# Weight conversions begun behind the 40th exponential instead of the 19th, and the MLP's work beside the attention eleven units later

## The chip, the cores and the metric

The kernel runs on one core of a Trainium2 chip. A core has TensorE (PE) for matrix products, VectorE (DVE), ScalarE (ACT), GpSimd (POOL) and SyncE (SP), whose queue issues the transfers. What is measured is the device time of one execution in microseconds, median of the runs.

## The reference, cut to what matters

Rotary attention, then two MLPs, each over the output of the one before:

```python
q_rot, k_rot = rotate(q), rotate(k)                # 4 batches, 8 heads, 576 tokens, 64 wide
attn = softmax(q_rot @ k_rot.T / sqrt(64))
x = (attn @ v)  ->  2304 tokens x 512
h = x @ w_in                                       # 512 x 2048
g = where(h >= 1, h, where(h <= -1, 0, (h + 1)**2 / 4))
x = g @ w_out                                      # 2048 x 512
h = x @ w_in2
out = (s * max(h, 0)**2 + b) @ w_out2
```

The MLP weights come as 64-bit floats.

## The kernel before, in words

Every matrix product of the MLPs is made of three: each operand is split into a high part (the operand cast to the fp32r type) and a low part, the rest, and high by high, high by low and low by high are summed. Turning one half (512 columns) of a weight slice from 64-bit floats into these two parts is a **conversion** (`Slice.convert`, called by `half`). It loads 512 KB (`load`, line 145), and then takes two ACT steps (line 134 at its start, line 139 for the high part), four DVE steps (lines 135 to 138, of 128 x 512) and two differences or sums on POOL, which the helper `pool_tt` (line 96) cuts in two pieces each (tiles `wm` and `w`). The raw data has two buffers, the scratch tiles `wa` and `wm` one.

The attention goes through 16 pairs of heads (`NPAIR`), four pairs for each batch, and each pair has nine **units** (`UNITS`), 144 in all. A unit takes its scores on TensorE (line 357), their maximum on DVE (`nm`, line 359), the exponential on ACT (`p`, line 364, kept in `exps`), transposes of the result (line 379) with copies by ACT or DVE, and, twice in a pair, the product with the values (`av`, lines 405 to 412). The scores have two buffers, and one comes free when its exponential is done. The rotation of the next pair's queries and keys (`rope_pair`, `lay_q`, `lay_k`) runs on POOL, DVE and ACT beside it (tiles `qin`, `kin`), and the laid keys go by transfers to `kh` and `kz`.

The unit loop traces, for each n, the five steps of `ORDER`: scores of unit n, loads and conversions (`do_load`), transposes, value products, and fill (`do_fill`). `issue_after(ins)` puts the instructions traced in its block behind `ins`, but only those on that instruction's own engine; for an exponential that is ACT. A planner then orders every engine's instructions ahead of time, by the order in which they were traced and by when it expects them to be ready, so an instruction may be issued before or behind others of its engine where no such bound stands. After that each engine takes its queue in order.

The **fill** is work of the first MLP that needs only tokens whose batch is finished. `beside(work)` is a generator for each batch but the last, and three shares come out of `ORDERS`: 2, 6 and 2 items. It issues the load and split of its first block of 288 tokens (`split_x`: tiles `xs`, `xh`, `xl`), then yields `LEAD` times with no work, and then one yield for each MLP unit: four first-layer units (`h`, 12 matmuls of line 181, and the activation) and four second-layer units (`y`, again 12 matmuls, line 181) for each item, 80 units in all. The first-layer units need the first half of four slices converted, the second-layer units the second half. `run_fill(budget)` takes steps from the generators:

```python
    def do_fill(n):
        if n < 48:
            return
        with tc.issue_after(exps[min(n, len(units)) - 4]):
            run_fill(0.62 if n < 76 else 0.92)
```

The loop runs n to 147, and `while fill: run_fill(1.0)` behind it traces what is left. A share is appended when the value product of its batch's last pair is traced, at n = 41, 75 and 111, and shares are taken one after the other.

Sixteen conversions prepare the eight slices of `set_a`, first halves and second halves of four slices and then of the other four. `convert()` takes the next. Nine of its calls stand at n = 33, 35, ... 49, the others at n = 70, 74, ... Eight more halves of later slices are converted and parked in memory from n = 96 on (`PARK_AT`). Behind the attention, `stage` goes on with the first MLP over the rest of the tokens (`hps`, `yps`), and the second MLP follows.

Of the kernel before, what the change touches and what calls it, by code (L numbers as in the profile page):

```python
# [36 lines left out]
RB = 2  # L37
XB = 3
N2 = 464
LEAD = 4  # L40
LT = 2
LA = 4
PB = 3
# [23 lines left out]
def kernel(ctx, tc, qq, kk, vv, tab, ww1, ww2, s, b, out):  # L67
# [45 lines left out]
    exps, tps, maxs = {}, {}, {}  # L113

    class Slice:
# [6 lines left out]
        def convert(self, raw, pools, hi, lo):  # L122
            if not wide:
                split(hi, lo, raw, nc.scalar, nc.gpsimd)
                return


            top = raw.bitcast(F32).rearrange("p (n t) -> p n t", t=2)[:, :, 1]
            low = raw.bitcast(U16).rearrange("p (n t) -> p n t", t=4)[:, :, 1]
            pool = pools[self.f * 2 + self.made & 1 if len(pools) > 1 else 0]  # L130
            a = pool.tile([P, HW], F32, tag="wa", name="wa", bufs=WB)
            m = pool.tile([P, HW], F32, tag="wm", name="wm", bufs=WB)
            au, mu = a.bitcast(U32), m.bitcast(U32)
            nc.scalar.activation(a, top, AF.Copy, scale=2.0 ** -112)
            nc.vector.tensor_scalar(out=mu, in0=au, scalar1=3, scalar2=None, op0=ALU.logical_shift_left)
            nc.vector.scalar_tensor_tensor(out=mu, in0=au, scalar=0x80000000, in1=mu, op0=ALU.bitwise_and, op1=ALU.bitwise_or)
            nc.vector.tensor_scalar(out=au, in0=mu, scalar1=0xFF800000, scalar2=None, op0=ALU.bitwise_and)
            nc.vector.scalar_tensor_tensor(out=a, in0=low, scalar=2.0 ** -36, in1=a, op0=ALU.mult, op1=ALU.mult)
            nc.scalar.copy(hi, m)  # L139
            pool_tt(out=m, in0=m, in1=hi, op=ALU.subtract)  # L140
            pool_tt(out=lo, in0=m, in1=a, op=ALU.add)
# [116 lines left out]
    def load_qk(i, nm, pieces=WHOLE):  # L258
        bb, hp = divmod(i, NP)
        t = att2.tile([P, 2, S], F32, tag="qkin", name=f"{nm}in", bufs=QB)  # L260
        for c in pieces:
            nc.sync.dma_start(out=t[:, :, c], in_=(qq if nm == "q" else kk)[bb, hp, :, :, c])
        qk_in[nm, i] = t

    def load_v(i):
        bb, hp = divmod(i, NP)
        t = att2.tile([P, 5, 2, D], F32, tag="vin", name="vin", bufs=VB)
        for out, src in ((t[:, :, 1], vv[bb, hp, :, :, 1]), (t[:D, :4, 0], vv[bb, hp, D:, :4, 0]), (t[D:, :4, 0], vv[bb, hp, :D, 1:, 0]), (t[D:, 4, 0], vv[bb, hp, :D, 0, 0])):
            nc.sync.dma_start(out=out, in_=src)
        v_in[i] = t  # L270
# [15 lines left out]
    def rope_pair(i, nm, mul, add, lo_eng, pieces=WHOLE):  # L286

        t = qk_in[nm, i]
        tt = {nc.gpsimd: pool_tt, nc.vector: nc.vector.tensor_tensor}
        last = None  # L290
        for c in pieces:
            tt[mul](out=t[:, :, c], in0=t[:, :, c], in1=tab_sb[:, :, c], op=ALU.mult)
            r = t[:, 1, c]
            tt[add](out=r, in0=t[:, 0, c], in1=r, op=ALU.add)
            last = (lay_q if nm == "q" else lay_k)(i, t, c, lo_eng)
        return last
# [4 lines left out]
    def lay_q(i, t, c, lo_eng, heads=range(2)):  # L301

        st = stacks["q", i] = qs_t[i % 2]
        r = t[:, 1, c]
        for j in heads:
            own, other = SELF[j], SELF[1 - j]
            at = slice(j * QW + c.start, j * QW + c.stop)
            h = nc.scalar.activation(st[own, at], r[own], AF.Copy, scale=0.125)
            m = nc.vector.scalar_tensor_tensor(out=st[other, at], in0=r[own], scalar=0.125, in1=st[own, at], op0=ALU.mult, op1=ALU.subtract)
        return h.ins, m.ins  # L310
# [153 lines left out]
    def split_x(c, again):  # L464
        xh = m1.tile([P, KD, N1], F32R, tag="xh", name="xh")
        xl = m1.tile([P, KD, N1], F32R, tag="xl", name="xl")
        if again:
            return load_parts((xh, xl), c * N1, N1)
        for k in range(KD):
            xs = m2.tile([P, N1], F32, tag="xs", name="xs", bufs=3)  # L470
            nc.sync.dma_start(out=xs, in_=xd[k, :, c * N1:(c + 1) * N1])
            split(xh[:, k, :], xl[:, k, :], xs, nc.scalar, nc.gpsimd)
        return xh, xl
# [3 lines left out]
    def beside(work):  # L477
        x = split_x(work[0][0], work[0][0] in kept)
        for _ in range(LEAD):
            yield 1.0  # L480
# [48 lines left out]
    def turned_by(t, c):  # L529
        nc.vector.tensor_tensor(out=t[:, :, c], in0=t[:, :, c], in1=tab_sb[:, :, c], op=ALU.mult)  # L530
        return nc.vector.tensor_tensor(out=t[:, 1, c], in0=t[:, 0, c], in1=t[:, 1, c], op=ALU.add).ins
# [53 lines left out]
    def do_load(n):  # L585
        if n == 0:
            with tc.issue_after(turned):
                turned_by(tq, QP[1])
                lay_q(0, tq, QP[1], None)
        elif n in (1, 2):  # L590
            with tc.issue_after(maxs[n]):
                if n == 1:
                    turned_by(tq, QP[2])
                else:
                    lay_q(0, tq, QP[2], None)
        if n < len(units):
            i, k = units[n]
            if i + 1 < NPAIR:
                if i == 0 and k in (2, 6):
                    with tc.issue_after(maxs[k]):  # L600
                        turned_by(qk_in["q", 1], HALVES[k // 6])
                if i == 0 and k in (4, 5, 7, 8):
                    with tc.issue_after(maxs[k]), tc.issue_after(exps[k - 1]):
                        lay_q(1, qk_in["q", 1], HALVES[k // 6], None, [int(k in (5, 8))])
                if i and k == 0:
                    with ExitStack() if i > 1 else tc.issue_after(parts[1][1]), ExitStack() if i > 1 else tc.issue_after(maxs[9]):
                        rope_pair(i + 1, "q", nc.gpsimd, nc.vector, None)
                elif k == 2:
                    with ExitStack() if i else tc.issue_after(exps[2]), ExitStack() if i else tc.issue_after(lowest):
                        rope_pair(i + 1, "k", nc.gpsimd, nc.gpsimd, [nc.gpsimd, nc.vector])  # L610
                elif k == 7:
                    load_v(i + 1)
                elif k in (4, 6) and i + 2 < NPAIR:
                    load_qk(i + 2, "q" if k == 4 else "k")

        if n in range(33, 51, 2) or n in range(70, 110, 4):
            with tc.issue_after(exps[n - 14]):
                convert()

        if n in PARK_AT and parking:  # L620
            with tc.issue_after(exps[n - 4]):
                parking.pop(0).park(wst, scratch)()
# [31 lines left out]
# [6 lines that stand above are left out]
    acts = {"q": do_qk, "l": do_load, "t": do_t, "a": do_av, "f": do_fill}  # L660
    for n in range(len(units) + LA):
        with ExitStack() as st:
# [541 lines left out]
```

## Time and profile before

| | us |
|---|---|
| median of 3 runs | 1116.79 |
| lowest and highest | 1115.44, 1121.0 |
| the profiled execution, its time | 1116.36 |
| its span, first to last instruction | 1114.6 |
| PE, DVE, ACT, POOL busy | 1071.6, 783.8, 626.7, 428.6 |
| first and last exponential begin | 15.2, 417.5 |
| first matmul of the fill begins | 132.9 |

The span is the time between the program's first and last instruction on the chip; the execution's own time is a little longer. Busy time of PE includes matmuls that overlap, so a PE that is always busy may still not be at its densest.

### The profile page before, as it was taken

The page shows a single profiled execution, that of the slowest core. Times are in us where ns is not written, and L with a number is a line of the kernel's source. Part 1 is how long each engine was busy: PE and PEld are TensorE (multiplying, and loading weights), DVE is VectorE, ACT ScalarE, POOL GpSimd, SP SyncE. Part 2 cuts the span into 40 slices and gives each one's busy share as a digit, 9 for nine tenths or more (in the row PEclk, how much of TensorE's full clock was granted, in tenths as well). Part 3 has the DMA queues.
Part 4 walks back from the last instruction along what each step waited for, and adds up shares of the span by engine and source line. Part 5 has one row for each costly group of instructions (what it writes and reads, how often), then busy time and mean ns, then how long its engine had stood idle before and what let it go on. Part 6 is the DMA issues. An engine that isn't in the chain of part 4 may idle for free.

```text
span 1114.6 us, 20055 instructions
## 1 busy us (share of the span) xinstructions
PE 1071.6 (96%) x7296; PEld 979.2 (88%) x7296; DVE 783.8 (70%) x1453; ACT 626.7 (56%) x1432; POOL 428.6 (38%) x564
## 2 busy tenths in 40 slices
PE   5898999999999999999999999999999999999998
PEld 4666787778888889999999999999999999999997
DVE  7989998887666663454657666867777778677754
ACT  5777877767656665454545445474555448334431
POOL 6988978785553332332544445110212110000000
PEclk9999999999999999999999999999999999999999
DMA  8665956665656544656465663231322843221220
GB/s 240 170 190 163 270 162 212 216 191 152 213 179 189 173 151 140 223 167 194 146 187 204 211 228 113 94 113 59 116 87 90 303 169 117 83 82 44 81 63 36
DMA packets 109762, 173.24 MB, mean 155 GB/s; under 512 B 29408, under 2 KB 80608, under 8 KB 109664
## 3 DMA queue, kind: packets, MB, share of 16 engines
q1 hardware_dynamic: 109664, 171.97, 49.0%
q8 instruction: 57, 0.93, 0.4%
q14 instruction: 41, 0.34, 0.1%
HBM read 110.10 MB, written 48.56 MB: 142 GB/s over the span
## 4 chain that ended last, share of the span: by engine, by line
PE 73%; DVE 8%; POOL 7%; DMA 6%; ACT 3%; issue 3%; SPq 0%; POOLq 0%; DVEq 0%; ACTq 0%
PE hps L181 14%; PE sum L940 14%; PE yps L856 6%; PE yps L854 6%; PE yps L855 6%; PE yps L790 4%; PE yps L791 4%; PE yps L792 4%; PE h L181 3%; PE sc L357 3%; PE y L181 3%; PE av L405 3%; POOL kin L96 3%; PE tp L379 2%; DVE nm L359 2%
## 5 line engine op out<-in xcount | busy, mean ns | idle before, releaser
L181 PE MATMUL hps<-xh,w 128*128 128x288 f32 (+4 forms) x640 | 163.4, 325 | 0.0
L364 ACT ACTIVATE p<-sc,nm 128x576 f32<-128x576 f32 x144 | 106.5, 741 | 40.6 <-DVE nm L359 35.7
L357 PE MATMUL sc<-kh,qs 128*128 128x288 f32 x336 | 102.6, 328 | 25.6 <-ACT p L364 14.8
L359 DVE TENSOR_REDUCE nm<-sc 128x1 f32<-128x576 f32 x144 | 106.8, 748 | 20.5 <-PE sc L357 19.8
L948 ACT ACTIVATE four<-four,b_sb,s_sb 128x480 f32<-128x480 f32 x64 | 47.4, 782 | 127.8 <-DVE four L947 127.8
L856 PE MATMUL yps<-gh,w 128*128 128x480 f32 (+1 forms) x320 | 118.6, 371 | 0.0
L854 PE MATMUL yps<-gh,w 128*128 128x480 f32 (+1 forms) x320 | 118.5, 370 | 0.0
L855 PE MATMUL yps<-gl,w 128*128 128x480 f32 (+1 forms) x320 | 118.5, 370 | 0.0
L181 PEld LDWEIGHTS hps<-xh,w 128*128 128x128 f32 x640 | 113.3, 188 | 1.0
L96 POOL TENSOR_TENSOR wm<-wm,w 128x256 f32<-128x256 f32 x80 | 67.8, 867 | 109.2 <-ACT w L139 62.3
L181 PE MATMUL hps<-xl,w 128*128 128x288 f32 (+4 forms) x320 | 103.7, 324 | 0.0
L357 PEld LDWEIGHTS sc<-kh,qs 128*128 128x128 f32 x336 | 63.3, 191 | 45.2 <-ACT p L364 26.3
L790 PE MATMUL yps<-gh,w 128*128 128x288 f32 (+3 forms) x288 | 93.2, 323 | 1.2 <-DVE yp L797 0.7
L357 PE MATMUL sc<-kz,qs 128*128 128x288 f32 x336 | 92.9, 299 | 0.0
L792 PE MATMUL yps<-gh,w 128*128 128x288 f32 (+3 forms) x288 | 92.9, 323 | 0.0
L791 PE MATMUL yps<-gl,w 128*128 128x288 f32 (+3 forms) x288 | 92.9, 323 | 0.0
L379 PE MATMUL tp<-ident,p 128*128 128x128 f32 x576 | 87.3, 276 | 2.6 <-DVE pt L386 1.8
L96 POOL TENSOR_TENSOR wm<-wm,raw 128x256 f32<-128x256 f32 x16 | 12.8, 820 | 175.1 <-ACT raw L139 175.1
L405 PE MATMUL av<-pt,vin 128*64 128x256 f32 (+1 forms) x512 | 75.1, 418 | 1.3 <-ACT pt L382 0.8
L181 PE MATMUL y<-gh,w 128*128 128x288 f32 x320 | 73.9, 303 | 1.4 <-ACT pt L382 0.4
L379 PEld LDWEIGHTS tp<-ident,p 128*128 128x128 f32 x576 | 70.1, 142 | 5.6 <-DVE pt L386 2.8
L181 PE MATMUL h<-xh,w 128*128 128x288 f32 x320 | 71.8, 301 | 2.9 <-DVE pt L386 2.1
(153 smaller groups left out, 2888.5 us busy)
## 6 DMA issues: line engine op xcount, KB each, us to landing
wraw<-in_ww SPq DMA_DIRECT2D x56, 512.0 KB, 4.2
w<-parkd SPq DMA_DIRECT2D x24, 512.0 KB, 6.1
kin<-in_k SPq DMA_DIRECT2D x15, 576.0 KB, 5.6
qin<-in_q SPq DMA_DIRECT2D x15, 576.0 KB, 5.1
kh<-kin SPq DMA_DIRECT2D x60, 144.0 KB, 3.1
parkd<-wraw SPq DMA_DIRECT2D x16, 512.0 KB, 3.2
xs<-y1d SPq DMA_DIRECT2D x32, 240.0 KB, 2.7
xd<-u SPq DMA_DIRECT2D x16, 288.0 KB, 2.6
```

The source lines that it names most:

```text
L96: m = nc.gpsimd.tensor_tensor(out=out[c], in0=in0[c], in1=in1[c], op=op)
L181: m = nc.tensor.matmul(out_ps, l, r, start=(i == 0), stop=(i == n - 1))
L357: nc.tensor.matmul(sc[:, half, o:o + n], l, r[:, k0:k0 + n], start=m == 0, stop=m == len(todo) - 1)
L359: maxs[i * 9 + k] = nc.vector.tensor_reduce(out=nm, in_=sc[:, :, :288], axis=AX.XY, op=ALU.max, negate=True).ins
L379: m = nc.tensor.transpose(v[:, c, :], p[:, c * P:(c + 1) * P], ident)
L790: nc.tensor.matmul(acc, wh, gh, start=f == 0, stop=False)
L791: nc.tensor.matmul(acc, wh, gl, start=False, stop=False)
L792: nc.tensor.matmul(acc, wl, gh, start=False, stop=last)
L854: nc.tensor.matmul(acc, wh, gh, start=f == 0, stop=False)
L855: nc.tensor.matmul(acc, wh, gl, start=False, stop=False)
L856: nc.tensor.matmul(acc, wl, gh, start=False, stop=last)
L940: nc.tensor.matmul(acc, l, r, start=j == 0, stop=j == len(t) - 1)
```

## The change

The generators of the fill yield eleven times with no work instead of four. The nine early calls of `convert` stand at n = 45, 47, ... 61, and the ACT steps of each are queued behind exponential n - 5 (the 40th to the 56th) instead of n - 14 (the 19th to the 35th). The later calls are as they were.

```diff
-LEAD = 4
+LEAD = 11
...
-        if n in range(33, 51, 2) or n in range(70, 110, 4):
-            with tc.issue_after(exps[n - 14]):
+        if n in range(45, 63, 2) or n in range(70, 110, 4):
+            with tc.issue_after(exps[n - 5 if n < 63 else n - 14]):
                 convert()
```

## Rows read from the trace of the kernel before

**Rows 1.** the page, span and busy time of each engine
```profile
span 1114.6 us, 20055 instructions
...
PE 1071.6 (96%) x7296; PEld 979.2 (88%) x7296; DVE 783.8 (70%) x1453; ACT 626.7 (56%) x1432; POOL 428.6 (38%) x564
```

**Rows 2.** windows: edges, length, busy us (instructions) per engine, clock, DMA
```profile
54.20:73.20 19.00, 18.03 (x133) 12.83 (x132) 17.36 (x29) 14.34 (x35) 14.61 (x19) 1.00 0.64 177
...
73.20:94.00 20.80, 18.84 (x137) 13.11 (x137) 18.88 (x32) 15.43 (x37) 17.86 (x26) 1.00 0.56 165
...
94.00:114.20 20.20, 18.00 (x131) 12.57 (x128) 18.37 (x30) 14.76 (x36) 17.79 (x24) 1.00 0.67 196
...
134.30:161.30 27.00, 24.70 (x193) 21.33 (x192) 24.60 (x42) 20.45 (x51) 25.71 (x34) 1.00 0.52 156
...
161.30:186.60 25.30, 23.16 (x176) 20.09 (x176) 20.03 (x35) 18.89 (x47) 17.84 (x24) 1.00 0.73 225
...
186.60:216.00 29.40, 28.10 (x227) 23.98 (x223) 24.35 (x44) 20.98 (x51) 22.84 (x30) 1.00 0.59 188
...
216.00:241.30 25.30, 22.23 (x163) 19.56 (x163) 20.89 (x37) 19.11 (x49) 19.11 (x27) 1.00 0.59 183
...
241.30:273.40 32.10, 29.43 (x231) 26.33 (x231) 24.85 (x45) 21.65 (x55) 21.83 (x29) 1.00 0.62 193
...
366.20:398.10 31.90, 31.68 (x250) 28.33 (x251) 19.02 (x38) 21.21 (x56) 12.23 (x18) 1.00 0.56 173
```

**Rows 3.** the same windows for line 357 alone, the score matmuls
```profile
73.20:94.00 20.80, 7.82 (x42) 5.76 (x42) 1.00 0.56 165
```

**Rows 4.** the same windows for line 181 alone, the MLP matmuls
```profile
134.30:161.30 27.00, 9.73 (x62) 8.31 (x61) 1.00 0.52 156
...
161.30:186.60 25.30, 9.46 (x62) 8.37 (x62) 1.00 0.73 225
...
186.60:216.00 29.40, 9.26 (x60) 8.30 (x60) 1.00 0.59 188
...
216.00:241.30 25.30, 10.52 (x68) 9.31 (x68) 1.00 0.59 183
...
241.30:273.40 32.10, 15.15 (x98) 13.43 (x99) 1.00 0.62 193
...
366.20:398.10 31.90, 16.38 (x108) 14.45 (x107) 1.00 0.56 173
```

**Rows 5.** chain of the whole run, one piece: start us, us, what
```profile
426.49 3.20 PE y L181 x24
```

**Rows 6.** chain of waits between 54 and 103 us, shares by line
```profile
by line: issue 16.6%; POOL kin L96 13.9%; DMA kz<-kin 10.5%; POOL qin L96 10.4%; POOL wm L96 6.7%; PE sc L357 6.1%; DVE nm L359 5.3%; POOL w L96 4.7%; PE av L405 3.6%; PE tp L379 3.0%; DMA kin<-in_k 2.9%; DVE wm L136 2.6%; DVE qs L309 2.5%;
```

**Rows 7.** instructions by line, 54 to 134 us: busy us, mean ns
```profile
L96 POOL TENSOR_TENSOR w<-wm,wa 128x256 fp32r<-128x256 f32 x10 | 7.9, 797 | 0.1
...
L96 POOL TENSOR_TENSOR wm<-wm,w 128x256 f32<-128x256 f32 x10 | 7.6, 779 | 1.9 <-DVE wa L137 1.9
...
L138 DVE SCALAR_TENSOR_TENSOR wa<-wraw,wa 128x512 f32<-128x512 uint16 x6 | 6.6, 1100 | 0.1
```

**Rows 8.** line 96 between 54 and 134 us, ns min/median/max
```profile
L96 POOL TENSOR_TENSOR kin<-kin,tab_sb x16: 783/801/1322, 66.8 to 126.8; 128x288 f32<-128x288 f32 x16
```

**Rows 9.** line 134, first ACT step of conversions, to 255 us
```profile
L134 ACT ACTIVATE wa<-wraw x16: 648/674/702, 55.8 to 246.0; 128x512 f32<-128x512 f32 x16
```

**Rows 10.** timeline of ACT, 110 to 186 us: start us, us
```profile
130.02 0.69 ACT L134 ACTIVATE wa<-wraw 128x512 f32<-128x512 f32 x1
...
185.18 0.69 ACT L134 ACTIVATE wa<-wraw 128x512 f32<-128x512 f32 x1
```

**Rows 11.** tile xh, 130 to 440 us: ns min/median/max, transfer landing
```profile
L96 POOL TENSOR_TENSOR xl<-xs,xh x21: 793/812/1247, 152.6 to 439.3; 128x288 fp32r<-128x288 f32 x21
...
DMA to landing us min/median/max: 3.4/4.5/8.1
```

**Rows 12.** waits of PE between 417 and 475 us
```profile
PE yps L790 <- ACT ys L507: 0.5, 1, 0.5
```

## The prediction

> **What bounds the kernel now.** I read the page first. TensorE is busy for 1071.6 of 1114.6 us, VectorE for 783.8, GpSimd for 428.6 [rows 1]. So nearly all of the span is matrix work that the change neither adds nor removes, and only stretches in which TensorE is not densely fed can pay or cost. To find them I cut the attention part into windows of nine attention units, one head pair each. The edges are the starts of every ninth exponential: 54.2 us is the 18th, 73.2 the 27th, then the 36th (94.0), 45th (114.2), 54th (134.3), 63rd, 72nd, 81st, 90th and 99th (273.4), and the row at 366.2 runs from the 126th to the 135th. Each such window holds 42 score matmuls, 4 for each of eight units and 10 for the unit of both heads' ends [rows 3].
>
> A window with MLP units in it must be freed of them before it can be compared. An MLP unit is 12 matmuls of line 181, and 24 of them took 3.20 us at a stretch [rows 5], so 1.6 us each unit where TensorE is dense. The window at 366.2 us is dense, busy 31.68 of 31.9 us [rows 2]. It holds 108 such matmuls [rows 4], 9 units or 14.4 us, which leaves **17.5 us for nine attention units, the floor**. The same subtraction over the other windows [rows 2, 4] gives 18.7 at 134.3, 17.0 at 161.3, 21.4 at 186.6, 16.2 at 216.0 and 19.0 at 241.3. The three windows with no MLP at all took 19.0, 20.8 and 20.2, mean 20.0 [rows 2]. So without filler nine units cost about 2.5 us over the floor. There VectorE is busy 91% of the time and GpSimd 77 to 88%, and TensorE's clock stays at 1.00, the level of 2.4 GHz [rows 2].
>
> Who holds up those windows? The chain of waits from 54 to 103 us runs through GpSimd's rotary work on `kin` and `qin` (24.3%), but also through the conversions: 6.7 and 4.7% in GpSimd's pieces for `wm` and `w`, 2.6% in VectorE's `wm` [rows 6]. That is 14.0% of 49 us, 6.9 us.
>
> **The change part by part.** No instruction is added or removed. Sixteen conversions of MLP weights start between 55.8 and 246.0 us [rows 9], 12.7 us apart in the mean. Four of them lie before the 40th exponential (which by the window edges starts near 103 us). The first nine now go behind the 40th to 56th, so these four leave the stretch. Their loads leave it too, from the third on, since the raw weights have two buffers and each further load waits for a conversion to end; on SyncE's queue they move behind the loads of the next pairs, and no exponential waits for them.
>
> The fill's budget follows from the code. Inside the unit loop it is 28 x 0.62 + 72 x 0.92 = 83.6 steps. Before, the first two shares take 4 + 16 and 4 + 48 of them, the third gets 11.6, 4 of them lead: 71.6 MLP units beside attention, 8.4 behind it. After, 11 + 16 and 11 + 48 are 86 already: 61.6 units beside attention, 18.4 behind. Ten units, 16 us of TensorE, move from attention to its tail; as dense work that is even, and only what each stretch loses or gains over the floor counts. The first MLP unit comes 7 / 0.62 = 11.3 units later, at the 66th instead of the 54th or 55th. The second share has a pause 7 / 0.92 = 7.6 units longer, about the 85th to the 97th. The third share's pause now lies behind the loop, where it takes no time.
>
> A, units 18 to 40 without conversions. At most the chain's 6.9 us come back, at least nothing, since GpSimd's rotary chain stands right behind. I take half, **-3.4 us**.
>
> B, units 54 to 66 without MLP, with conversions. Before, nine at 18.7 and three at the rate of 17.0, together 18.3 for nine. After, I take the 20.0 of the windows that also hold conversions and no MLP: 1.7 x 12 / 9 = **+2.3 us**. Ends: nothing, and 20.8 against 17.0, +5.1.
>
> C, the longer pause of the second share. The windows from 186.6 to 273.4 average 18.9 freed of MLP; 20.0 - 18.9 over 7.6 units is **+0.9 us**. Ends: nothing, and 20.8 against 16.2, +3.9.
>
> D, ten more MLP units behind attention. In the tail before, TensorE waited 0.5 us in all between 417 and 475 us [rows 12], because the third share's input had been loaded and split long before. Now its four transfers and splits are issued with no lead. A transfer of this tile takes 4.5 us to land, and four low parts on GpSimd 4 x 0.81 us [rows 11], 7.7 us together. The work that hides it is the 2.4 last units of the second share, 3.8 us, and the last units' transposes and value products. Without the latter 3.9 us stand open, with them none; I take **+2.0 us**.
>
> The parked weights, the next stage and everything behind it keep their work and order; the conversions end some 20 us later, while the first weights of the second half are due only after the fill's 27 + 11 + 16 steps, beyond the 110th unit. I cost them at nothing.
>
> Sum: -3.4 + 2.3 + 0.9 + 2.0 = +1.8 us. The profiled execution took 1116.36 us, 1.8 over its span and 0.4 under the median of 1116.79. That gives 1118.2 for it and, carried to the median, **1118.6**. Ends of all terms: -6.9 and +12.9.
>
> **The rivals.** First, GpSimd is the true limit and filler hides conversions later for nothing. A conversion holds GpSimd for 2 x (797 + 779) ns = 3.2 us [rows 7], and while it shares the stretch its neighbours stretch too: the rotary pieces of one shape took 783 to 1322 ns [rows 8]. The whole 6.9 us would come back and B to D be nothing: 1116.4 - 6.9 = **1109.5**. It decides once A, less B to D, is over 5.6 us. Against it: the floor leaves 2.5 us for nine units, 6 us for the 22 units, so A would have to reach the floor. The Trainium skill (SBUF — State Buffer, "Who interferes with whom") says that a VectorE instruction with two SBUF inputs and a reading GpSimd instruction exclude each other for the whole instruction; two of a conversion's VectorE steps are such, the one at line 138 with a mean of 1100 ns [rows 7], and the spread on GpSimd agrees with it. By that rule a conversion costs GpSimd up to 2.2 us more than its own pieces, which speaks for this rival and is why it has a chance above one in ten.
>
> Second, slower: the conversions come too late for the first second-layer units. These need eight. Where conversions followed one another without pause, six started from 130.02 to 185.18 us [rows 10], 11.0 us apart. Starting near 100 us, the eighth starts at 177 and is done some 8 us later, at 185. The first such unit is due after 26 units at 20.0 for nine (58 us), and 6.5 more with four MLP units (20.8 us): 179 us. The stall would be 6 us, and where the order on TensorE's queue is fixed nothing behind it can pass. 1118.6 + 6 = **1125**. It decides once the spacing is over 10.2 us. Against it: without MLP activations on the engines the spacing may shrink, and the order may be laid so that attention fills in.
>
> Third, the pauses are hidden and A is as small as they are: within a microsecond or two of before. That is the forecast's own neighbourhood, and I count it there.
>
> **How the numbers follow.** A measurement here can tell about 0.5%, 5.6 us, from no change: below 1111.2 is faster, above 1122.4 slower. The forecast (all small terms, nothing decides) 0.52, of which 0.04 spills over each bound; the first rival 0.20; the second 0.20; a tail or pause at its dear end (D or C, +5 to +12) 0.08, of which 0.02 stays within the bounds. So faster is 0.04 + 0.20 = 0.24, slower 0.04 + 0.20 + 0.06 = 0.30, and the same 0.44 + 0.02 = 0.46. The range from 1109.5, the first rival, to 1128, near the upper end of the terms, leaves out about 0.2.
>
> **What would show it.** A: the first conversion near 100 us instead of 55.8, and the 36th exponential 2 to 5 us before 94.0. B: no line 181 before some 155 us, and nine units at about 20 us up to there. C: a second stretch without line 181 near the 85th to 97th unit. D: some 18 to 20 MLP units behind the last exponential, with TensorE's waits for `xh` or `xl` there up to 4 us. The forecast is wrong if windows without MLP run near 17.5 us once conversions are gone (then faster), or if line 181's second-layer matmuls wait for conversions (then slower).

## The result, and the profile after

The changed kernel takes 1126.83 us (median of 6 runs, 1124.07 to 1130.43), the kernel before 1117.69 us beside it (6 runs). The ratio is 1.0087, 95% interval 1.0070 to 1.0105: **slower by about 9.7 us**. That lies inside the stated range, above the likeliest time by 8. The profiled execution took 1130.43 us, the slowest of the six, so sums over its trace come out some 3 or 4 us too large.

The page, span and busy time:

```profile
span 1128.7 us, 20086 instructions
...
PE 1077.5 (95%) x7296; PEld 984.6 (87%) x7296; DVE 783.2 (69%) x1453; ACT 628.4 (56%) x1432; POOL 428.6 (38%) x564
```

TensorE has the same work within 6 us [rows 1], spread over 14 us more. The windows below are nine attention units each, by the same exponentials as before: the edges are the starts of the 18th, 27th, 36th, 45th, 54th, 63rd and, last row, 90th. The columns are as in [rows 2].

```profile
57.10:74.70 17.60, 17.19 (x127) 12.18 (x124) 14.19 (x24) 13.41 (x33) 12.45 (x18) 1.00 0.48 134
...
74.70:93.70 19.00, 18.05 (x132) 12.55 (x130) 13.94 (x24) 12.67 (x31) 11.29 (x17) 1.00 0.50 141
...
93.70:116.80 23.10, 20.21 (x151) 14.18 (x151) 18.46 (x30) 15.60 (x40) 16.15 (x21) 1.00 0.61 167
...
116.80:137.60 20.80, 18.00 (x145) 13.95 (x141) 19.39 (x34) 15.53 (x37) 19.07 (x25) 1.00 0.84 258
...
137.60:160.80 23.20, 18.38 (x132) 14.99 (x132) 19.52 (x33) 15.38 (x36) 17.56 (x26) 0.93 0.60 174
...
160.80:187.50 26.70, 23.61 (x183) 20.14 (x182) 24.05 (x42) 20.17 (x52) 23.45 (x30) 1.00 0.47 138
...
243.80:269.20 25.40, 21.01 (x151) 17.00 (x150) 19.49 (x36) 16.23 (x40) 16.82 (x24) 0.93 0.61 171
```

Line 181 alone in two of them, as in [rows 4]:

```profile
160.80:187.50 26.70, 8.41 (x56) 7.66 (x56) 1.00 0.47 138
...
243.80:269.20 25.40, 2.01 (x14) 1.93 (x15) 0.93 0.61 171
```

First, units 18 to 36, now free of conversions, took 17.6 and 19.0 us against 19.0 and 20.8 [rows 2]: 3.2 us gained, and the first of them runs at the floor. The next nine, where the conversions now begin, lost 2.9 us again (23.1 against 20.2). Second, the three windows with conversions and no MLP took 23.1, 20.8 and 23.2, mean 22.4, where I had put 20.0 for those from the 54th unit on. Third, the second share's pause: 25.4 us less 14 matmuls of 181 (1.9 us) leaves 23.5 for nine units, against 19.0 before. Last, TensorE's clock column reads 0.93 in two of these rows, where it read 1.00 in every row of before.

The first step of the conversions, as in [rows 9]; 20 here, since the window is longer and holds parked ones too:

```profile
L134 ACT ACTIVATE wa<-wraw x20: 649/676/741, 102.9 to 328.2; 128x512 f32<-128x512 f32 x20
```

TensorE's largest wait between 15 and 500 us, in the changed kernel and then in the one before (total us, times, longest us):

```profile
PE sc L357 <- ACT p L364: 22.2, 22, 3.7
```

```profile
PE sc L357 <- ACT p L364: 14.8, 17, 1.9
```

Most of the extra waiting, 7.4 us, is in the scores, which wait for an exponential to free their buffer. No matmul of the fill waits for a converted weight: there is no such row in this list. Last, the tail, in windows from the last value product to about the end of the fill's last matmul, changed kernel and before:

```profile
428.60:467.00 38.40, 37.89 (x285) 37.65 (x284) 10.56 (x26) 20.39 (x58) 11.95 (x16) 1.00 0.63 200
```

```profile
432.00:456.00 24.00, 23.46 (x175) 23.23 (x176) 7.26 (x17) 13.57 (x38) 9.54 (x12) 1.00 0.72 222
```

Both are as good as full, 37.9 of 38.4 and 23.5 of 24.0 us.

**One stop followed back.** TensorE has two stops of 3.7 us. The first ends at 150.2 us. This is the chain of waits in front of it (start us, us, what):

```profile
140.27 2.85 issue
...
144.94 2.02 POOL qin L96 x2
...
146.98 1.33 DVE qin L294
...
149.35 0.84 ACT p L364 x2
...
150.23 0.81 PE sc L357 x4
```

The score waits for an exponential, that for a maximum, that stands on VectorE behind the addition `qin` of line 294, and the addition waits for GpSimd. This is the timeline of GpSimd there, with its idle time in brackets:

```profile
143.16 3.79 POOL L96 TENSOR_TENSOR qin<-qin,tab_sb 128x288 f32<-128x288 f32 x4 [2.89 <-DMA qin<-in_q]
```

GpSimd had nothing for 2.9 us because a query load had not landed. On SyncE's queue this load (line 262) was issued right behind a raw weight load (line 145):

```profile
133.24 1.27 SPq L329 DMA_DIRECT2D kz<-kin  x2
136.93 0.35 SPq L145 DMA_DIRECT2D wraw<-in_ww  x1
...
137.38 0.38 SPq L262 DMA_DIRECT2D qin<-in_q  x1
```

And this is why it was late, a row of SyncE's own waits between 100 and 160 us:

```profile
SPq L145 <- DVE wa L138: 5.4, 3, 2.7
```

The weight load stood at the head of the queue until a conversion's last VectorE step gave its buffer back (at line 138), 5.4 us in three times; here 2.4 us, from the end of the issue before it at 134.5. The query that came late belongs to a pair whose scores are due more than a dozen units later, but its addition had its place in VectorE's queue ahead of maxima that were due at once. Two windows of 5 us show what follows:

```profile
145.00:150.00 5.00, 1.58 (x14) 1.34 (x12) 3.55 (x6) 1.24 (x3) 5.00 (x6) 1.00 0.67 202
...
150.00:155.00 5.00, 4.77 (x26) 4.74 (x27) 3.25 (x6) 4.54 (x14) 4.86 (x9) 0.66 0.07 24
```

In the first, TensorE is busy for 1.6 of 5 us; in the second it has work again for 4.8 us, at a mean clock of 0.66, part of it at 1.2 instead of 2.4 GHz. The second stop, from 253.7 to 257.4 us, looks the same on VectorE, which waited 3.6 us for GpSimd in front of such an addition. What held up the query there was not followed:

```profile
254.13 1.33 DVE L294 TENSOR_TENSOR qin<-qin 128x576 f32<-128x576 f32 x1 [3.62 <-POOL qin L96]
```

### The profile page after: what moved, and what is told of

Read it like the earlier page. It is cut to its first block, busy times and chain, and to the rows that moved or that the text cites. A ratio compares the mean times of both kernels' runs of the same rounds, so it can differ in the third digit from the quotient of the medians.

```text
span 1128.7 us, 20086 instructions
## 1 busy us (share of the span) xinstructions
PE 1077.5 (95%) x7296; PEld 984.6 (87%) x7296; DVE 783.2 (69%) x1453; ACT 628.4 (56%) x1432; POOL 428.6 (38%) x564
## 4 chain that ended last, share of the span: by engine, by line
PE 75%; DVE 7%; DMA 6%; POOL 6%; issue 3%; ACT 3%; SPq 1%; POOLq 0%; ACTq 0%; DVEq 0%
PE hps L181 14%; PE sum L940 13%; PE yps L856 6%; PE yps L855 6%; PE yps L854 6%; PE y L181 5%; PE h L181 4%; PE yps L790 4%; PE yps L791 4%; PE yps L792 4%; PE sc L357 4%; PE av L405 3%; PE tp L379 2%; POOL kin L96 2%; POOL qin L96 2%
## 5 line engine op out<-in xcount | busy, mean ns | idle before, releaser
L357 PE MATMUL sc<-kh,qs 128*128 128x288 f32 x336 | 106.3, 338 | 33.3 <-ACT p L364 22.2
L96 POOL TENSOR_TENSOR wm<-wm,w 128x256 f32<-128x256 f32 x80 | 71.3, 911 | 114.8 <-ACT w L139 72.1
L357 PE MATMUL sc<-kz,qs 128*128 128x288 f32 x336 | 95.6, 305 | 0.0
L107 DVE TENSOR_TENSOR gl<-hps,gh 128x288 fp32r<-128x288 f32 (+4 forms) x88 | 46.4, 527 | 39.2 <-ACT gh L103 39.0
```

What stands on the lines that cost most here:

```text
L96: m = nc.gpsimd.tensor_tensor(out=out[c], in0=in0[c], in1=in1[c], op=op)
L357: nc.tensor.matmul(sc[:, half, o:o + n], l, r[:, k0:k0 + n], start=m == 0, stop=m == len(todo) - 1)
```

## The experiments

Ratios are to the kernel before, run on the same chip, with 95% intervals. "Lead" is the number of empty steps ahead of a share.

**The two parts alone, and the pauses one by one.** In the last two, and in those below that say so, the shares have leads of their own:

```diff
-LEAD = 4
+LEAD = 11                      # first run: leads alone, conversions as before
...
-LEAD = 11
+LEAD = 4                       # second run: moved conversions alone
...
-        for _ in range(LEAD):
+        for _ in range(LEADS[work[0][0]]):     # by the share's first block: 0, 2, 4
+LEADS = {0: 11, 2: 4, 4: 4}    # third run, on the changed kernel
+LEADS = {0: 4, 2: 11, 4: 4}    # fourth run, on the kernel before
```

> LEAD 11, conversions as before. Pause theory (attention units without filler are bound by the rotary chain, so every unit that loses its filler costs): about 8 to 11 us over before, as much as the whole change or more, since the 3 us that early units gained without conversions are missing. Late-conversion theory (second-layer units wait for their weights): the conversions are early here, so within 2 us of before.

Measured: 1.0065 (1.0045 to 1.0085), 1122.47 us. So the leads alone make most of the loss, short of the 8 to 11 us that I expected, and far from nothing.

> Conversions behind the 40th to 56th exponential, LEAD 4 as before. Pause theory: the early units gain 3 us; the filler that starts at the 54th unit must wait for its weights, which makes one unplanned pause: 0 to 5 us over before. Late-conversion theory: the most lateness of all variants, 9 us over before or more.

Measured: 1.0179 (1.0146 to 1.0212), 1135.54 us, about 20 us over. Here the rival holds. TensorE's waits between 15 and 500 us in this run:

```profile
PE y L181 <- POOL w L96: 9.4, 5, 3.2
...
PE y L181 <- ACT w L139: 2.8, 2, 1.7
```

Second-layer matmuls waited 12.2 us for converted weights. The longer lead hides this: neither the changed kernel nor the third run has such a wait among its longest.

> The whole change, but only the first share of the fill has 11 empty steps, the second and third have 4. Pause theory: the pause at about the 85th to 97th unit shrinks to four or five units and most of its 9 us (profiled executions) comes back: 1 to 5 us over before. Late-conversion theory: as the whole change, 9 us over before, since the conversions are where they were.

Measured: 1.0086 (1.0061 to 1.0111), 1125.41 us. A miss for the pause theory: taking the second pause back gave nothing that can be measured, though the profile of the changed kernel had shown nine units at 23.5 us there. The number is the one that the late-conversion theory gave, but in this run too no matmul of the fill waits for a weight.

> The kernel before with 11 empty steps for the second share alone. Pause theory: 4 to 8 us over before, from one longer pause near the 78th to 90th unit. Late-conversion theory: nothing is late, so within 2 us of before.

Measured: 1.0017 (0.9999 to 1.0035), 1116.89 us. The second pause alone costs about 2 us, and nothing is not excluded. My 4 to 8 had been read off one window of one execution; a window that loses 4.5 us is paid back by its neighbours, as the changed kernel's units 108 to 117 (27.6 us with 8 MLP units, so 15 without) show.

**The first pause, with the conversions where they were.**

> Conversions as before, 11 empty steps for the first share alone. If the shares' pauses add (both shares together cost 7 us, the second alone 2), this costs about 5 us over before. If the second share's pause is what costs with both, about nothing. With the conversions moved the same pause cost 10 us, so a result near 5 leaves 5 us to the conversions' move itself.

Measured: 1.0054 (1.0037 to 1.0071), 1122.24 us, 6 us over before, as expected if the pauses add (6 + 2 against 7). The pause itself ran at the old pace, 20.0 and 20.2 us for nine units. The loss came where the filler began: the next nine took 29.9 us with 54 matmuls of line 181 (7.2 us), so 22.7 without them, against 17.0 before. It holds 126 matmuls of other lines, that of before 114.

```profile
156.20:186.10 29.90, 25.87 (x180) 22.58 (x181) 23.34 (x42) 20.66 (x53) 20.37 (x27) 0.89 0.56 160
```

Pieces of the chain of waits there:

```profile
170.54 1.38 POOL w L96 x2
...
171.94 0.67 ACT wa L134
...
176.45 3.26 PE h L181 x12
```

And TensorE in three windows of 4 us (columns as in [rows 2]):

```profile
168.00:172.00 4.00, 3.19 (x26) 2.96 (x24) 0.79 (x2) 2.29 (x9) 3.94 (x8) 1.00 0.09 20
...
172.00:176.00 4.00, 1.77 (x8) 1.71 (x8) 3.36 (x7) 3.97 (x10) 2.20 (x4) 0.71 0.00 0
...
176.00:180.00 4.00, 3.86 (x17) 3.53 (x16) 3.91 (x8) 3.56 (x9) 2.43 (x3) 0.50 0.55 125
```

TensorE stood still for 3.0 us, up to 174.2, for a copy of line 382 on ACT. This is ACT's queue in front of that copy, with its idle time in brackets:

```profile
170.57 0.67 ACT L321 CAST kin<-kin 128x576 fp32r<-128x576 f32 x1 [1.32 <-POOL kin L96]
...
171.94 0.66 ACT L134 ACTIVATE wa<-wraw 128x512 f32<-128x512 f32 x1 [0.39 <-POOL w L96]
...
173.61 0.57 ACT L382 COPY pt<-tp 128x512 f32<-128x512 f32 x1
```

A cast of a later pair's keys waited 1.32 us for GpSimd, and a conversion's first step (`wa`) 0.39 us more, until GpSimd had done with the one scratch tile. Activations of the filler that had just begun stood between them and the copy. Then the clock was 0.71 and 0.50, and the first 12 matmuls of an MLP unit took 3.26 us instead of 1.6 [rows 5].

**Is TensorE idle in the pause?** On that run, seven of the empty steps get matmuls whose result is thrown away:

```diff
-        for _ in range(LEADS[work[0][0]]):
+        for m in range(LEADS[work[0][0]]):
+            if m >= 4:
+                ps = ps_f.tile([P, 512], F32, tag="bank", name="idle")
+                accumulate(ps[:, :N1], [(x[0][:, 0, :P], x[0][:, k % KD, :]) for k in range(12)], CF)
             yield 1.0
```

> As the run with 11 empty steps for the first share alone, but the last seven of these steps each take 12 matmuls whose result nobody reads: 7 x 1.6 = 11.2 us of work thrown away on TensorE, in the very units that lost their filler. If TensorE stands idle there because nothing else is ready, part of it costs nothing: 4 to 8 us over that run instead of 11. If the empty units are as dense as filled ones and the pause costs elsewhere, the full 11 us.

Measured: 1.0083 (1.0060 to 1.0106), 1126.9 us: about 3 us over that run for 11.2 us of matmuls (0 to 6 by the two intervals), at or under the low end of the 4 to 8. So some 8 us of this work cost nothing in the whole run. But the pause did not have 8 us to give: TensorE's busy time in the same 20 us (second number), first without and then with this work, is 17.2 and 19.4 us, so that only 3.0 us were idle there:

```profile
136.00:156.20 20.20, 17.18 (x133) 13.44 (x132) 18.93 (x33) 14.74 (x36) 19.27 (x26) 1.00 0.52 156
```

```profile
136.00:156.20 20.20, 19.41 (x151) 16.91 (x153) 16.63 (x24) 12.49 (x28) 18.34 (x25) 1.00 0.37 110
```

By units the picture is clearer. Units 54 to 63 took 27.8 us with the extra work, 7.6 more than without. The eighteen units behind them took 53.5 us instead of 59.8 (first row with it, second without), for nearly the same work. What was delayed in the pause was made up behind it:

```profile
135.00:162.80 27.80, 26.05 (x203) 22.36 (x202) 22.91 (x38) 16.73 (x38) 22.26 (x29) 1.00 0.50 150
162.80:216.30 53.50, 50.74 (x386) 44.67 (x386) 44.63 (x73) 39.12 (x99) 42.52 (x55) 0.97 0.56 172
```

```profile
156.20:216.00 59.80, 53.49 (x394) 46.69 (x395) 46.72 (x80) 40.44 (x101) 42.21 (x56) 0.94 0.59 176
```

**The blocked queue.** On the changed kernel, the rotation's addition may not stand ahead of the maximum three units back:

```diff
-                    with ExitStack() if i > 1 else tc.issue_after(parts[1][1]), ExitStack() if i > 1 else tc.issue_after(maxs[9]):
+                    with ExitStack() if i > 1 else tc.issue_after(parts[1][1]), ExitStack() if i > 1 else tc.issue_after(maxs[9]), tc.issue_after(maxs[n - 3]) if n >= 54 else ExitStack():
```

> The whole change, and from the 54th unit on VectorE's part of the next query's rotation may not stand ahead of the maximum three units back. In the changed kernel that addition waited for a query load, which stood behind a weight load waiting for its buffer on SyncE's queue, and TensorE stood still for 3.7 us. Theory of the blocked queues: the stops over 3 us near 145 us go, and 2 to 5 us of the change's 9 come back. Theory that unfilled units are simply bound by their own work: no difference from the changed kernel within 2 us, and the stall turns up elsewhere.

Measured: 1.0058 (1.0043 to 1.0073), 1122.77 us: some 3 us of the 9.7 come back, with an interval that just touches that of the changed kernel. The scores' waits fell as well:

```profile
PE sc L357 <- ACT p L364: 16.6, 21, 3.0
```

It was 22.2 us in 22 waits, and neither stop of 3.7 us is left (the one of 3.0 us lies near 42 us, where no edit reaches). But most of the 3 us was not won at the stop near 145 us. Units 54 to 63 took 20.8 us instead of 23.2, and the next nine 28.5 instead of 26.7, with 56 matmuls of line 181 in either kernel. That is 0.6 us for the eighteen; where the rest came from was not traced:

```profile
136.00:156.80 20.80, 18.59 (x132) 14.45 (x132) 19.42 (x31) 15.54 (x36) 18.19 (x25) 0.92 0.64 190
156.80:185.30 28.50, 24.85 (x186) 20.66 (x186) 24.91 (x46) 20.46 (x52) 23.15 (x30) 1.00 0.53 169
```

The same edit on the kernel before:

> The kernel before with the rotation's VectorE part held three units back from the 54th unit on. If the blocked maximum was a fault of the changed kernel's order on SyncE alone, no difference within 2 us. If it is a general fault of the order, 1 to 3 us faster than before, and faster than both kernels.

Measured: 1.0000 (0.9979 to 1.0022), 1116.72 us. So holding the addition back gains nothing there that can be measured, as the first theory said.

**The other direction.** Leads of 0 for all shares, then for the second and third alone, both on the kernel before (`LEAD = 0`; `LEADS = {0: 4, 2: 0, 4: 0}`):

> The kernel before with no empty step at all, so that all three shares start earlier. If each empty unit costs, as 7 steps more in each share cost 7 us, 4 steps fewer give 2 to 4 us, unless the first units then wait for their weights (the rival: lateness, 0 to 5 us slower than before).

Measured: 1.0154 (1.0137 to 1.0170), 1134.18 us.

> The kernel before with 4 empty steps for the first share and none for the second and third. If a pause costs by its length, 0.5 to 1.5 us faster than before, which may be under what can be measured; if the pause is needed to load and split the next share's input, 1 to 3 us slower.

Measured: 1.0116 (1.0089 to 1.0142), 1129.4 us. Neither theory had this size. Two rows of the last run tell of it, TensorE's wait between 270 and 360 us and its window behind the attention:

```profile
PE y L182 <- DVE gl L108: 7.5, 2, 5.2
```

```profile
451.00:470.00 19.00, 13.97 (x71) 12.09 (x68) 2.72 (x7) 7.12 (x19) 6.46 (x9) 0.73 0.87 282
```

Without a lead the second-layer matmuls wait for activations (7.5 us), and with the fill used up early only 4.3 MLP units, not 13.2, are left for the time behind the last exponential. TensorE is then busy for 14.0 of 19 us at a clock of 0.73, where it was full before. How the 13 us divide between the two was not tried.

**Between and beyond.** First, on the kernel before, `LEADS = {0: 7, 2: 4, 4: 4}`; then its first nine conversions six exponentials earlier, `exps[n - 20 if n < 63 else n - 14]`:

> Conversions as before, 7 empty steps for the first share instead of 4 (11 cost 6 us). If a missing filler unit costs by its number, 3 / 7 of it, 2.5 us over before. If there is a best point between, 0 or less.

Measured: 0.9976 (0.9959 to 0.9993), 1115.43 us. Not 2.5 us slower: there is a best point between 4 and 11.

> The kernel before with the first nine conversions allowed six exponentials earlier (n - 20). If units without filler suffer from conversions (term A), the early units lose up to 3 us and later ones gain as much: within 2 us of before. If lateness of the weights binds the kernel before already, 1 to 4 us faster.

Measured: 0.9973 (0.9958 to 0.9989), 1113.92 us. About 3 us faster, the opposite of what the change does. This run and the one before it are the fastest here, 0.3 and 0.2% under the kernel before; between the two the intervals do not decide, and they were not tried together. Its units 18 to 36 took 17.8 and 17.9 us, as little as the changed kernel's, although two conversions start in them (at 62.0 and 77.9 us). So what the changed kernel gained there need not come from the absence of conversions:

```profile
58.10:75.90 17.80, 17.43 (x129) 12.40 (x128) 16.94 (x29) 14.16 (x34) 16.10 (x22) 1.00 0.71 195
75.90:93.80 17.90, 17.90 (x133) 12.77 (x132) 16.61 (x29) 14.58 (x35) 16.84 (x23) 1.00 0.66 187
```

## Why the prediction was right or wrong

The direction of the sum and the range held; the likeliest case, within 0.5%, did not come true. That the range held is partly luck: its upper end was made of the dear ends of B, C and D, but C stayed near its price and D was nothing, while moved conversions that cost time, and stops with a lower clock behind them, were in no term of the sum. By its steps:

- **A was right where it was looked for and wrong as a term.** Units 18 to 40 gained 3.1 us (54.2 to 102.3 us before, 57.1 to 102.2 after), against 3.4 forecast. By the 45th unit the gain was gone: units 18 to 45 took 59.7 us against 60.0. The move of the conversions as a whole did not gain: on top of the first lead it cost 3.6 us (1.0086 against 1.0054), on top of all leads 2.5, both with intervals that overlap. The step that failed is the sentence that the loads move behind the next pairs' loads and no exponential waits for them. Issue itself costs little, but a load that waited for its buffer held up the loads behind it; through GpSimd and VectorE an exponential did wait. What this wait costs alone is not shown: the run with the addition held back was about 3 us faster, but only 0.6 us of that lies in the units around the stop that was followed. That the weight load was to blame is read from the trace; no run moved it.
- **B was mis-sized**, +2.3 for what measured 6 us alone. I had priced an empty unit by the windows of before and these were right for the pause itself (20.2 us). What I left out is the loss where the filler starts: 22.7 against 17.0 us for nine units, with a stop of 3.0 us and half the clock behind it. With the conversions moved in, units 54 to 63 took 23.2 us. I had read the clock's 1.00 [rows 2] as a property of unfilled units and gave a fall no place among the rivals, although TensorE's stops there were already near 2 us. The Trainium skill (TensorE: Matmul & The Clock Gate, "HAM oscillation — how this bites in real kernels") tells of a matmul kernel in which each long wait for a transfer throttles the array, so that the next piece of work starts slow. Here the wait was for ACT, and the 3.26 us for 12 matmuls agree.
- **C was right**: +0.9 forecast, +1.9 measured with an interval from 0 to 3.9, and nothing on the changed kernel. Its ends were not what I took them for, since the windows of [rows 2, 4] do not hold the same attention work, nor 42 score matmuls each (38 to 46): without line 181 the one at 186.6 has 227 - 60 = 167 matmuls, the one at 216.0 only 163 - 68 = 95, and the one of the floor 250 - 108 = 142. Much of the 21.4 and the 16.2 is work that fell into one window instead of the next.
- **D was too dear**: 2.0 forecast, and the tail is full, 0.5 us idle in either kernel, with 23.5 MLP units behind the last exponential (I had 18 to 20) where before had 13.2. The last transposes and value products were presumably the better cover.
- **The first rival** (the whole 6.9 us come back) is refuted: the unfilled units with conversions took up what the early ones gave. Its sign came half true, 17.6 and 19.0 us for windows without conversions, and the kernel was slower all the same.
- **The second rival** named a real mechanism. With a lead of 4 the moved conversions made line 181 wait 12.2 us and cost 20 us. With the lead of 11 no such wait is left, although the eighth conversion ran from 191.4 to 203.5 us, later still than the 177 to 185 that I had worked out: the planner had laid TensorE's order around it. The matmuls of the first four second-layer units are spread from 185.2 to 204.2 us, where before they took 149.4 to 167.5.

Measured piece by piece: the first lead 6.0, the second 1.9, the moved conversions on both 2.5, together 10.4 against 9.7. In the prediction's terms this is B, C and A with its sign turned, in the order of the sum above. How much of B is stops and how much the clock was not separated; as an estimate, the two windows at 0.71 and 0.50 lost at most 4 x (0.29 + 0.50) = 3.2 us to the clock.

## What to carry to other kernels

Filler that moves from a loop to its tail is not even when the loop can take it in for less than its own time: of 11.2 us of thrown-away matmuls some 8 cost nothing here, and equally a tail that has run out of filler stands empty. When background work is moved, look through each in-order queue for what waits at its head (a load for its buffer, an early rotation for its load, a cast for GpSimd) and who stands behind it. And read a window's loss only together with its neighbours: nine units at 23.5 us looked like 4.5 us of loss, and undoing them changed nothing.

## What the runs showed of the hardware that had not been expected

A stop of TensorE of 3.0 to 3.7 us inside a loop that is otherwise busy was followed by a stretch at the lower clock; where the fill began it fell just on the filler that came next. It also happens where no edit reaches: this is the run with the longer second lead, whose first 56 us are the program of before, and its pause (columns as in [rows 2]):

```profile
33.40:56.00 22.60, 19.44 (x132) 13.85 (x130) 18.02 (x29) 14.27 (x35) 22.18 (x28) 0.92 0.59 169
...
217.00:238.80 21.80, 17.84 (x128) 14.64 (x129) 19.14 (x32) 14.78 (x35) 18.20 (x24) 0.92 0.65 193
```

Its units 9 to 18 ran at 0.92 and took 22.6 us, while in the profiled execution of before the same units ran at 1.00 and took 21.3. The changed kernel's 23.1 us there are therefore no effect of the change. Of the fourteen profiled executions twelve show this fall, between 40 and 43 us, and that of before is one of the two without, which makes its units 9 to 18 look about 2 us better than theirs.

Shorter stops were followed by a fall too: the two above come behind stops of 2.8 and 2.0 us. And in the run with the moved conversions alone, a stop of 2.8 us at the first place was followed by none:

```profile
33.50:54.50 21.00, 17.84 (x132) 12.66 (x128) 17.99 (x28) 14.17 (x35) 20.74 (x27) 1.00 0.64 183
```
